# The low halves of layer 2's last float32r operands made by GpSimd or VectorE, in a new planned order

## The chip, the cores and the metric

The kernel runs on one core of one Trainium2 chip. The metric is the device time of one execution in microseconds. The engines are called by the profile's names: PE is TensorE's matmuls and PEld its weight loads, DVE is VectorE, ACT is ScalarE, POOL is GpSimd and SP is SyncE, whose queue issues all DMAs.

## What is computed

Top-32 attention over 4 batches of 8 heads, 576 tokens of 64 dimensions, then two MLPs over the 2304 tokens. All in float32.

```python
def _attn_ref(q, k, v):
    scores = scale * np.matmul(q, k.transpose(0, 1, 3, 2))
    kth = np.partition(scores, -top_k, axis=-1)[..., -top_k:-top_k + 1]
    scores = np.where(scores >= kth, scores, -1000000000.0)
    attn = np.exp(scores - np.max(scores, axis=-1, keepdims=True))
    attn = attn / (np.sum(attn, axis=-1, keepdims=True) + 1e-09)
    return np.matmul(attn, v).astype(np.float32)
...
x = np.ascontiguousarray(attn_out.transpose(0, 2, 1, 3)).reshape(B * S, H * D)   # 2304 x 512
h = x @ w_in                                     # layer 1: 512 -> 2048
x = (h * (1.0 / (1.0 + np.exp(-1.702 * h)))) @ w_out
...
h = x @ w_in                                     # layer 2: 512 -> 2048
P = a[0] + a[1] * h + a[2] * h2 + a[3] * h3      # h2 = h*h, h3 = h2*h
Q = 1.0 + np.abs(b[0]) * np.abs(h) + np.abs(b[1]) * h2
return ((P / (Q + 1e-06)) @ w_out).astype(np.float32)
```

## The kernel before

**Tiles.** The tokens are 18 tiles of 128. A tile has 8 heads, so there are 144 attend steps. One step is: score matmuls into a PSUM buffer S (L678); four MAX8 on DVE (L689) with three MATCH_REPLACE8 between them (L693), which find the 32nd largest value; three ACT passes (L696, L698, L700) and a subtraction on POOL (L702), which make the weights as a high and a low float16 half in A; a transposing DMA from A to AT; and the value matmuls (L721). One small POOL operation per step is L691.

**Layers.** The tiles are grouped in nine granules of two. Layer 1 of a granule runs in units of 512 columns: matmuls into the PSUM buffer h (L860), tanh on ACT (L880), a gate on DVE (L893), halves gh and gl (L917 on ACT, L919 on POOL), and matmuls into acc0 and acc1 (L954). Layer 2's unit has 24 matmuls into h, four ACT passes that read h (L880: Abs, Square and two affine ones), one operation on DVE (L888), Ln and Exp on ACT (L906, L907), three products or sums of two 128x512 tiles on POOL or DVE (L884 is the POOL form, L885 the DVE form of the same line), which give the gate M, and the output matmuls (L951 in plain float32). There is one PSUM buffer for h (NH=1).

**float32r.** For the last two granules (RG = (7, 8)) the output matmuls of layer 2 run in float32r: `round_split` splits the gate tile (names E) and the two weight tiles of a unit (K the high, V the low half) into a rounded high half (L817 on ACT, L818 the DVE form) and the low remainder (L819), and L938 does three matmuls where L951 does one of a slower kind. This makes 16 units with three splits each, 48 in all. They are the last stage of the program.

**Order.** Each engine runs its instructions in the order of the program. `Program.schedule` sets that order: every operation is recorded with an engine, a planned duration and a priority, and perhaps `alt`, another engine that may take it. The planner plays the program through with these durations and picks for each engine the operation that can start first, weighed by its priority and the table OFF. `lock` says that an operation keeps DVE and POOL from running such operations at the same time in the plan. The line that the change is about reads before:

```python
op("DVE", dve(512), lambda: lo(DVE), [rd, hb], [lb], prio, lock=True)
```

`dve(512)` plans 0.6 us for it.

Of the kernel before, what the change touches and what calls it, by code (L numbers as in the profile page):

```python
# [223 lines left out]
def kernel(  # L224
# [20 lines left out]
    NPAIR = DFF // 256  # L245
# [14 lines left out]
    op = pr.op  # L260
# [120 lines left out]
    def w_load(layer, f2, prio):  # L381
        for j in range(2):
# [70 lines left out]
            if layer == 1:  # L453
                dg = buf("dg", [P, P], F32, NDG)
                op("POOL", PDIAG, lambda dg=dg, sc=sc: POOL.tensor_scalar(dg.t, eye, sc, None, ALU.mult), [scb], [dg], prio)
                for c in range(2):
# [6 lines left out]
                    op("PE", 6 * 0.2155, rest, [low, dg, dst], [pl[c]], prio)  # L463
# [21 lines left out]
    def w_consts(layer, prio):  # L485
# [10 lines left out]
        if layer == 1:  # L496
            op("DVE", 1.0, one, [wscale[j, f2] for f2 in range(NPAIR) for j in range(2)], [wcb[1]], prio)
        else:
            op("DVE", 0.15, lambda: DVE.tensor_scalar(sc2, wsi[:, :, 2], im1, 1.0 / CG, ALU.mult, ALU.mult),
               [wcb[1]] + [wscale[2, f2] for f2 in range(NPAIR)], [wcb[2]], prio)  # L500
# [163 lines left out]
    def attend(i, prio):  # L664
# [7 lines left out]
        for r0, n, bb, _ in reversed(sg):  # L672
# [7 lines left out]
            op("PE", 0.49, mm, [qs, K], [s], prio - 1)  # L680
# [129 lines left out]
    def round_split(src, cols, rd, tags, prio):  # L810
# [9 lines left out]
        op("DVE", dve(512), lambda: lo(DVE), [rd, hb], [lb], prio, lock=True)  # L820
# [296 lines left out]
RG = (7, 8)  # L1117
NT0 = 8
# [3 lines left out]
LAV = 0.8762  # L1122
# [11 lines left out]
KLAG = 7.5819  # L1134
QLAG = 3.1885
NKH = 1
NQH = 1
W1P = -0.0003
W2P = 7.8782
W1R = 0.02  # L1140
W2R = 1.0078
LATE = 2
MLAG = 3.5653
SWITCH = 53.68
OLAG = 2.4023
UW = 1.1408
ALATE = -51.37
OFF = {
    ('attend', 'ACT'): 15.52,
    ('attend', 'ACT', 0): -8.51,  # L1150
    ('attend', 'ACT', 1): 15.81,
    ('attend', 'ACT', 2): -8.72,
    ('attend', 'ACT', 3): 6.94,
    ('attend', 'ALT'): 7.89,
    ('attend', 'DVE'): 33.66,
    ('attend', 'DVE', 0): 0.07,
    ('attend', 'DVE', 1): -0.32,
    ('attend', 'DVE', 2): -2.5,
    ('attend', 'DVE', 3): 0.86,
    ('attend', 'PE'): -272.38,  # L1160
    ('attend', 'PE', 0): 3.52,
    ('attend', 'PE', 1): -15.49,
    ('attend', 'PE', 2): 9.83,
    ('attend', 'PE', 3): 17.15,
    ('attend', 'POOL'): 12.13,
    ('attend', 'POOL', 0): -0.38,
    ('attend', 'POOL', 1): -34.1,
    ('attend', 'POOL', 2): 30.8,
    ('attend', 'POOL', 3): -23.18,
    ('attend', 'SP'): -111.84,  # L1170
    ('attend', 'SP', 0): -11.92,
    ('attend', 'SP', 1): 0.05,
    ('attend', 'SP', 2): 8.26,
    ('attend_av', 'ACT'): -323.75,
    ('attend_av', 'ACT', 0): -26.14,
    ('attend_av', 'ACT', 1): 3.65,
    ('attend_av', 'ACT', 2): -17.11,
    ('attend_av', 'ACT', 3): -11.88,
    ('attend_av', 'PE'): -84.87,
    ('attend_av', 'PE', 0): 2.96,  # L1180
    ('attend_av', 'PE', 1): -3.29,
    ('attend_av', 'PE', 2): -12.39,
    ('attend_av', 'PE', 3): -3.81,
    ('k_prep', 'ACT'): 4.12,
    ('k_prep', 'ACT', 0): 14.56,
    ('k_prep', 'ACT', 1): -56.64,
    ('k_prep', 'ACT', 2): 20.72,
    ('k_prep', 'ALT'): 64.83,
    ('k_prep', 'DVE'): 30.23,
    ('k_prep', 'DVE', 0): -43.96,  # L1190
    ('k_prep', 'DVE', 1): -88.43,
    ('k_prep', 'DVE', 2): 22.15,
    ('k_prep', 'DVE', 3): -2.16,
    ('k_prep', 'PE'): 49.18,
    ('k_prep', 'PE', 0): 5.15,
    ('k_prep', 'PE', 1): 5.28,
    ('k_prep', 'PE', 2): 68.78,
    ('k_prep', 'PE', 3): 5.95,
    ('k_prep', 'POOL'): -32.59,
    ('k_prep', 'POOL', 0): 18.63,  # L1200
    ('k_prep', 'POOL', 1): -4.97,
    ('k_prep', 'POOL', 2): -26.89,
    ('k_prep', 'POOL', 3): -30.93,
    ('k_prep', 'SP'): 58.29,
    ('k_prep', 'SP', 0): 6.33,
    ('k_prep', 'SP', 1): -71.47,
    ('k_prep', 'SP', 2): 35.83,
    ('k_prep', 'SP', 3): 17.13,
    ('o_done', 'ACT'): -281.01,
    ('o_done', 'ACT', 0): 2.63,  # L1210
# [254 lines left out]
RATE = 2.25  # L1465
# [32 lines left out]
```

## Time and profile before

| | us |
|---|---|
| median of 3 runs | 1249.11 |
| lowest and highest | 1246.3, 1251.24 |
| the profiled execution | 1240.5 |
| its span, first to last instruction | 1238.8 |
| PE, DVE, ACT, POOL busy in it | 1095.7, 1096.0, 1032.0, 873.2 |

Busy time is a mean over stages with different limits; the rows below cut it by stages. The profiled execution is 8.6 us under the median, so a sum made on the profile is applied to the median as a difference.

### The profile page before, as it was taken

To read this page: it belongs to the slowest core of one execution; us is meant where nothing else is said; L and a number is where in the kernel's file an instruction comes from. 1 tells how busy PE (TensorE), PEld (TensorE's weight loads), DVE (VectorE), ACT (ScalarE), POOL (GpSimd) and SP (SyncE) were. 2 spreads that over 40 slices of the span, in tenths; PEclk is the share of its full clock that TensorE was granted. 3 is DMA by queue.
4 is the path that set the end of the run, shared out by engine and by line. 5 is a ranking of instruction groups with operands and counts; after the bars stand their busy time and mean duration, and the time that the engine had idled before them with its cause. 6 is when DMAs were issued, how large, how long until landed. Compare 5 with 4: busy or idle time off the path is not lost.

```text
span 1238.8 us, 26369 instructions
## 1 busy us (share of the span) xinstructions
PE 1095.7 (88%) x9290; PEld 744.2 (60%) x9290; DVE 1096.0 (88%) x2328; ACT 1032.0 (83%) x1917; POOL 873.2 (70%) x1230
## 2 busy tenths in 40 slices
PE   3867556868898999999989999999999999999997
PEld 2434243645565766676657765756676677677775
DVE  5879999999999999999999999969999999542886
ACT  5888888968888889999988888777889978856886
POOL 6887889886777679777785687556757856422765
PEclk9987678869899999999999999999999999999999
DMA  9949798889889649969695589656956863841651
GB/s 293 259 118 233 221 295 211 218 205 202 181 194 225 112 104 218 208 119 190 152 239 125 119 195 185 125 134 174 189 103 148 202 129 87 208 113 35 190 188 65
DMA packets 363845, 214.08 MB, mean 173 GB/s; under 512 B 316352, under 2 KB 328640, under 8 KB 363712
## 3 DMA queue, kind: packets, MB, share of 16 engines
q1 hardware_dynamic: 363712, 212.39, 71.8%
q8 instruction: 73, 1.20, 0.4%
q14 instruction: 60, 0.49, 0.1%
HBM read 127.93 MB, written 13.11 MB: 114 GB/s over the span
## 4 chain that ended last, share of the span: by engine, by line
PE 46%; DVE 21%; ACT 12%; POOL 8%; DMA 7%; issue 5%; SPq 1%; DVEq 0%; POOLq 0%; ACTq 0%
PE h L860 19%; PE acc L954 9%; PE acc L951 7%; DVE E L693 6%; DVE mx L689 5%; DMA AT<-A 4%; ACT t L880 4%; PE S L678 3%; PE misc L721 3%; POOL t L884 2%; DVE m L689 2%; PE acc L460 2%; PE acc L938 2%; POOL A L702 2%; ACT E L696 1%
## 5 line engine op out<-in xcount | busy, mean ns | idle before, releaser
L689 DVE MAX8 mx<-E 128x8 f32<-128x576 f32 x432 | 321.1, 752 | 3.7
L884 POOL TENSOR_TENSOR t<-t,t 128x512 f32<-128x512 f32 x155 | 211.2, 1363 | 70.6 <-ACT t L880 44.3
L702 POOL TENSOR_TENSOR A<-E,A 128x576 f16<-128x576 f32 x144 | 189.8, 1318 | 50.0 <-ACT A L700 40.7
L951 PE MATMUL acc<-ring,t 128*128 128x512 f32 x448 | 216.3, 608 | 5.3 <-DVE t L885 2.2
L860 PE MATMUL h<-xh,W 128*128 128x128 f16 (+1 forms) x2688 | 212.8, 238 | 6.3 <-DVE t L893 5.8
L693 DVE MATCH_REPLACE8 E<-mx,E 128x576 f32<-128x576 f32 x288 | 213.6, 742 | 0.0
L860 PE MATMUL h<-yh,ring 128*128 128x256 f16 x1728 | 205.0, 274 | 7.3 <-ACT t L880 6.8
L860 PEld LDWEIGHTS <-W 128*128 128x128 f16 x2688 | 192.1, 100 | 32.1 <-issue 12.3
L860 PEld LDWEIGHTS <-ring 128*128 128x128 f16 x1728 | 169.0, 98 | 54.6 <-issue 30.3
L954 PE MATMUL acc<-W,gh 128*128 128x512 f16 x576 | 173.9, 384 | 0.1
L678 PE MATMUL S<-K,qs 128*128 128x288 f16 (+1 forms) x640 | 110.1, 300 | 34.5 <-ACT E L696 32.9
L698 ACT ACTIVATE E<-E,nm,ei 128x576 f32<-128x576 f32 x144 | 124.3, 865 | 8.5 <-POOL nm L697 6.8
L919 POOL TENSOR_TENSOR gl<-t,gh 128x512 f16<-128x512 f32 x72 | 84.5, 1174 | 66.0 <-ACT gh L917 63.7
L689 DVE MAX8 m<-S 128x8 f32<-128x576 f32 x144 | 108.7, 755 | 23.1 <-PE S L678 17.3
L721 PEld LDWEIGHTS <-AT 128*128 128x128 f16 (+3 forms) x2400 | 90.2, 102 | 63.9 <-DMA AT<-A 47.2
L696 ACT ACTIVATE E<-S,mx 128x576 f32<-128x576 f32 x144 | 106.3, 739 | 21.6 <-DVE mx L689 21.2
L721 PE MATMUL misc<-V,AT 128*128 128x65 f16 (+6 forms) x2400 | 98.6, 197 | 28.4 <-DMA AT<-A 26.1
L880 ACT ACTIVATE t<-h,cf 128x512 f32<-128x512 f32 x144 | 93.8, 683 | 31.6 <-PE h L860 30.2
L951 PEld LDWEIGHTS acc<-ring,t 128*128 128x128 f32 x448 | 77.5, 191 | 69.3 <-issue 54.8
L954 PE MATMUL acc<-W,gl 128*128 128x512 f16 x288 | 110.3, 383 | 5.3 <-POOL gl L919 5.1
L678 PEld LDWEIGHTS <-qs 128*128 128x128 f16 (+1 forms) x640 | 63.5, 103 | 79.4 <-issue 60.4
L693 DVE MATCH_REPLACE8 E<-m,S 128x576 f32<-128x576 f32 x144 | 107.6, 747 | 0.0
(186 smaller groups left out, 2062.2 us busy)
## 6 DMA issues: line engine op xcount, KB each, us to landing
ring<-scr SPq DMA_DIRECT2D x144, 512.0 KB, 4.2
ring<-in_moe_w_out_dram SPq DMA_DIRECT2D x12, 1024.0 KB, 6.5
ring<-in_moe_w_in_dram SPq DMA_DIRECT2D x9, 1024.0 KB, 7.1
ld<-in_v_dram SPq DMA_DIRECT2D x32, 256.0 KB, 3.8
out_dram<-t SPq DMA_DIRECT2D x18, 256.0 KB, 2.9
lq<-in_q_dram SPq DMA_DIRECT2D x32, 128.0 KB, 3.4
ld<-in_k_dram SPq DMA_DIRECT2D x16, 256.0 KB, 3.8
yh<-in_moe_w_in_dram SPq DMA_DIRECT2D x4, 1024.0 KB, 6.3
```

Of the source, the lines that this page charges most:

```text
L678: PE.matmul(s[:n, c, :SH], qs[:, 2 * (h % 4) + x, :n], K[:, h % 2, c * SH:(c + 1) * SH], start=(x == 0), stop=(x == 1))
L689: op("DVE", dve(S, not r) + 0.02, lambda r=r, mv=mv: DVE.max(mv(), w.t if r else sv()), [w if r else s], [m], prio)
L693: op("DVE", dve(S, not r) + 0.085, lambda r=r, mv=mv: DVE.match_replace(w.t if r else two(w.t), mv(), w.t if r else sv(), NEG), [m, w if r ...
L696: op("ACT", act(S, True) + APA + 0.02, lambda: ACT.activation(two(e.t), sv(), AF.Prelu, bias=mx[:, 2, 7:8], scale=-1.0, alpha=NEAR), [s, m ...
L698: op("ACT", act(S) + 0.2, lambda: ACT.activation(e.t, e.t, AF.Exp, bias=nm[:, 1:2], scale=eb(0)), [e, nm, ei], [e], prio)
L702: lo = lambda en: en.tensor_tensor(A[:, 1, :S], e.t, A[:, 0, :S], ALU.subtract)
L721: PE.matmul(ps[r0:r0 + n, :hi - lo], at[:kp, x, j, r0:r0 + n], V[:kp, h % 2, j, lo:hi], start=(j == 0 and lo == D and x == 0), stop=(j == ...
L860: PE.matmul(o, w[:, half, kd * 256 + jj * P: kd * 256 + (jj + 1) * P], xy[:, tl, l * ND + kd, :], start=(kd == 0 and n == 0), stop=(kd == ...
L880: op("ACT", act(w, True) + APA, lambda f2=f2, c=c: ACT.activation(dst[:, c], src[:, c], func, bias=bias(f2) if bias else 0.0, scale=sc(f2) ...
L884: op("POOL", pool_tt(512), lambda: POOL.tensor_tensor(o.t, x.t, y.t, f), [x, y], [o], prio, alt=("DVE", dve(512) + 0.04, lambda: DVE.tenso ...
L951: PE.matmul(acc[j].t, u.gate[:, c], w[:, jj * DM:(jj + 1) * DM], start=st, stop=sp)
L954: PE.matmul(acc[j].t, l[:, c], w[:, half, jj * DM:(jj + 1) * DM], start=(st and n == 0), stop=(sp and n == 2))
```

## The change

The lows of `round_split` get a choice: POOL with a planned 1.35 us, or DVE with 1.2 us. Three other planned durations are raised. The planner's table of numbers is replaced as a whole, so that all operations of the program may stand in another order.

```diff
-                    op("PE", 6 * 0.2155, rest, [low, dg, dst], [pl[c]], prio)
+                    op("PE", PREST, rest, [low, dg, dst], [pl[c]], prio)
...
-            op("DVE", 1.0, one, [wscale[j, f2] for f2 in range(NPAIR) for j in range(2)], [wcb[1]], prio)
+            op("DVE", 2.5, one, [wscale[j, f2] for f2 in range(NPAIR) for j in range(2)], [wcb[1]], prio)
...
-            op("PE", 0.49, mm, [qs, K], [s], prio - 1)
+            op("PE", PES, mm, [qs, K], [s], prio - 1)
...
-        op("DVE", dve(512), lambda: lo(DVE), [rd, hb], [lb], prio, lock=True)
+        op("POOL", PLR, lambda: lo(POOL), [rd, hb], [lb], prio, alt=("DVE", DLR, lambda: lo(DVE)))
...
+PLR, DLR, PREST, PES = 1.35, 1.2, 1.6, 0.52
...
-LAV = 0.8762
+LAV = 2.0021
...
-SWITCH = 53.68
+SWITCH = 101.44
...
-    ('u_act2', 'DVE'): -136.15,
+    ('u_act2', 'DVE'): -149.57,
...
-RATE = 2.25
+RATE = 16.09
```

No instruction is added or dropped; some stand on another engine, and most stand elsewhere.

**PE, in the last stage.** h_2120 and h_2131 are the h tiles of the eighth and ninth of the sixteen units; the rows are the end of the one group of matmuls and the beginning of the next. Before, with the last five of the twelve output matmuls between:

```order
L938 MATMUL acc0_69<-V_2130_16181,E_2103_16141 128x512
L938 MATMUL acc0_69<-K_2129_16098,E_2104_16157 128x512
L938 MATMUL acc1_70<-K_2129_16098,E_2103_16141 128x512
L938 MATMUL acc1_70<-V_2130_16181,E_2103_16141 128x512
L938 MATMUL acc1_70<-K_2129_16098,E_2104_16157 128x512
L860 LDWEIGHTS ring_90
L860 MATMUL h_2131_16213<-yh_91,ring_90 128x256
```

After:

```order
L860 MATMUL h_2120_16132<-yh_91,ring_90 128x256
L860 LDWEIGHTS ring_90
L860 MATMUL h_2120_16132<-yh_91,ring_90 128x256
L860 LDWEIGHTS ring_90
L860 MATMUL h_2131_16181<-yh_91,ring_90 128x256
```

The twelve L938 between the two groups stand behind the second one now, in a block of 27.

**POOL, at the end of the program.** t_2202 and t_2213 are the gate tiles of the last two units, V_2209 to V_2228 weight lows of the last four units. Before, the last six rows that compute:

```order
L884 TENSOR_TENSOR t_2202_16658<-t_2202_16658,t_2201_16651 128x512
L884 TENSOR_TENSOR t_2202_16658<-t_2202_16658,t_2203_16665 128x512
L884 TENSOR_TENSOR t_2202_16658<-t_2202_16658,t_2200_16646 128x512
L884 TENSOR_TENSOR t_2213_16722<-t_2213_16722,t_2212_16717 128x512
L884 TENSOR_TENSOR t_2213_16722<-t_2213_16722,t_2214_16728 128x512
L884 TENSOR_TENSOR t_2213_16722<-t_2213_16722,t_2211_16711 128x512
```

After, the last nine:

```order
L819 TENSOR_TENSOR V_2209_16692<-ring_90,K_2208_16540 128x512
L819 TENSOR_TENSOR V_2218_16702<-ring_90,K_2217_16565 128x512
L884 TENSOR_TENSOR t_2213_16704<-t_2213_16704,t_2212_16697 128x512
L884 TENSOR_TENSOR t_2213_16704<-t_2213_16704,t_2214_16709 128x512
L819 TENSOR_TENSOR V_2220_16730<-ring_90,K_2219_16608 128x512
L819 TENSOR_TENSOR V_2222_16736<-ring_90,K_2221_16626 128x512
L819 TENSOR_TENSOR V_2224_16741<-ring_90,K_2223_16668 128x512
L819 TENSOR_TENSOR V_2226_16753<-ring_90,K_2225_16718 128x512
L819 TENSOR_TENSOR V_2228_16761<-ring_90,K_2227_16726 128x512
```

The weight lows came to POOL, five of them behind the last unit's products; the third product of a unit went to DVE.

**DVE, in the middle of the last stage.** t_2132 to t_2134 and t_2143 to t_2145 belong to the ninth and tenth unit. Before:

```order
L888 SCALAR_TENSOR_TENSOR t_2132_16247<-t_2133_16262,ab_76,t_2132_16247 128x512
L885 TENSOR_TENSOR t_2134_16272<-t_2134_16272,t_2133_16262 128x512
L819 TENSOR_TENSOR V_2165_16297<-ring_90,K_2164_16286 128x512
L819 TENSOR_TENSOR E_2126_16318<-t_2123_16201,E_2125_16295 128x512
L888 SCALAR_TENSOR_TENSOR t_2143_16315<-t_2144_16322,ab_76,t_2143_16315 128x512
L819 TENSOR_TENSOR E_2137_16357<-t_2134_16272,E_2136_16339 128x512
L819 TENSOR_TENSOR V_2174_16376<-ring_90,K_2173_16313 128x512
L819 TENSOR_TENSOR V_2176_16396<-ring_90,K_2175_16367 128x512
L888 SCALAR_TENSOR_TENSOR t_2154_16381<-t_2155_16389,ab_76,t_2154_16381 128x512
L819 TENSOR_TENSOR E_2148_16410<-t_2145_16327,E_2147_16398 128x512
```

After:

```order
L888 SCALAR_TENSOR_TENSOR t_2132_16220<-t_2133_16228,ab_76,t_2132_16220 128x512
L885 TENSOR_TENSOR t_2134_16254<-t_2134_16254,t_2133_16228 128x512
L885 TENSOR_TENSOR t_2134_16254<-t_2134_16254,t_2135_16265 128x512
L885 TENSOR_TENSOR t_2134_16254<-t_2134_16254,t_2132_16220 128x512
L888 SCALAR_TENSOR_TENSOR t_2143_16310<-t_2144_16318,ab_76,t_2143_16310 128x512
L885 TENSOR_TENSOR t_2145_16330<-t_2145_16330,t_2144_16318 128x512
L885 TENSOR_TENSOR t_2145_16330<-t_2145_16330,t_2146_16334 128x512
L885 TENSOR_TENSOR t_2145_16330<-t_2145_16330,t_2143_16310 128x512
```

Here the six lows went to POOL, and all three products of a unit came to DVE.

## Rows read from the trace of the kernel before

**Rows 1.** The page: busy time, and PE's granted clock in 40 slices.

```profile
PE 1095.7 (88%) x9290; PEld 744.2 (60%) x9290; DVE 1096.0 (88%) x2328; ACT 1032.0 (83%) x1917; POOL 873.2 (70%) x1230
...
PEclk9987678869899999999999999999999999999999
```

**Rows 2.** Busy time in stretches: us, PE, PEld, DVE, ACT, POOL, clock, DMA share, GB/s.

```profile
44.00:768.20 724.20, 619.13 (x5382) 413.81 (x5380) 691.27 (x1591) 632.11 (x1208) 570.57 (x837) 0.92 0.81 188
768.20:1052.40 284.20, 279.38 (x2527) 190.94 (x2528) 261.70 (x524) 234.94 (x422) 182.32 (x251) 1.00 0.66 145
1052.40:1130.00 77.60, 77.60 (x694) 52.78 (x693) 34.60 (x54) 51.15 (x96) 25.27 (x25) 1.00 0.49 129
1130.00:1239.00 109.00, 97.54 (x611) 74.62 (x608) 82.12 (x90) 85.78 (x144) 64.82 (x45) 1.00 0.40 136
```

**Rows 3.** What writes m, in one stretch (DVE, POOL); then what uses S.

```profile
768.20:1052.40 284.20, 63.22 (x121) 14.77 (x40) 1.00 0.66 145
...
L678 PE MATMUL S<-K,qs x640: 282/286/448, 42.9 to 1051.5; 128*128 128x288 f16 x144, 128*64 128x288 f16 x16
```

**Rows 4.** Timeline of PE in the last stage: start, us, line, tiles, count [idle before].

```profile
1155.24 2.78 PE L860 MATMUL h<-yh,ring 128*128 128x256 f16 x24
...
1160.71 2.78 PE L860 MATMUL h<-yh,ring 128*128 128x256 f16 x24 [1.29 <-ACT t L880]
...
1178.11 2.78 PE L860 MATMUL h<-yh,ring 128*128 128x256 f16 x24
...
1184.71 2.78 PE L860 MATMUL h<-yh,ring 128*128 128x256 f16 x24 [1.03 <-ACT t L880]
...
1189.36 0.74 PE L938 MATMUL acc<-K,E 128*128 128x512 f32 x2 [1.39 <-DVE E L819]
...
1203.42 2.78 PE L860 MATMUL h<-yh,ring 128*128 128x256 f16 x24 [0.61 <-ACT t L880]
```

**Rows 5.** Timeline of ACT between two of those groups.

```profile
1181.51 0.71 ACT L906 ACTIVATE t<-t,kc 128x512 f32<-128x512 f32 x1
...
1182.69 0.62 ACT L907 ACTIVATE t<-t 128x512 f32<-128x512 f32 x1
```

**Rows 6.** Timeline of DVE and POOL; two groups of 1130 to 1239 us: busy, mean ns, idle.

```profile
1154.63 0.68 DVE L819 TENSOR_TENSOR V<-ring,K 128x512 fp32r<-128x512 f32 x1
...
1157.11 1.77 DVE L819 TENSOR_TENSOR V<-ring,K 128x512 fp32r<-128x512 f32 x1
...
1142.96 1.28 POOL L884 TENSOR_TENSOR t<-t,t 128x512 f32<-128x512 f32 x1 [4.59 <-ACT t L880]
...
1154.59 8.68 POOL L884 TENSOR_TENSOR t<-t,t 128x512 f32<-128x512 f32 x5 [2.36 <-ACT t L880]
1163.71 1.29 POOL L884 TENSOR_TENSOR t<-t,t 128x512 f32<-128x512 f32 x1 [0.43 <-ACT t L907]
...
L884 POOL TENSOR_TENSOR t<-t,t 128x512 f32<-128x512 f32 x41 | 62.4, 1522 | 30.9 <-ACT t L880 21.0 <-ACT t L907 6.9 <-ACT K L817 0.7
...
L919 POOL TENSOR_TENSOR gl<-t,gh 128x512 f16<-128x512 f32 x1 | 1.2, 1153 | 4.1 <-ACT gh L917 4.1
```

**Rows 7.** Timeline of the end: POOL's last products, PE's last matmul, the store.

```profile
1225.93 4.67 POOL L884 TENSOR_TENSOR t<-t,t 128x512 f32<-128x512 f32 x3 [0.56 <-ACT t L880]
...
1234.61 0.40 PE L938 MATMUL acc<-K,E 128*128 128x512 f32 x1
...
1234.97 1.03 SPq L1018 DMA_DIRECT2D out_dram<-t  x2
```

**Rows 8.** The chain that ended last: two of its pieces.

```profile
1035.54 2.62 PE h L860 x24
...
1129.84 2.59 PE acc L954 x12
```

**Rows 9.** DVE's waits, from 44 to 350 us and from 350 to 1090: us, times, longest.

```profile
DVE m L689 <- PE S L678: 8.2, 7, 3.2
...
DVE m L689 <- PE S L678: 9.1, 16, 1.8
```

More of the change, by code (lines that the diff above doesn't have):

```diff
@@ L1133 @@
 VLO = 0
[L1134 to L1135 removed]
+KLAG = 7.3553
+QLAG = 3.5241
 NKH = 1
 NQH = 1
[L1138 to L1141, printed above, removed]
+W1P = -0.5495
+W2P = 7.2247
+W1R = 0.672
+W2R = 0.9283
 LATE = 2
[L1143 to L1454 removed]
@@ L1464 @@
 WIN = {'DVE': 0.0, 'ACT': 0.0, 'POOL': 0.0, 'PE': 0.0, 'SP': 0.0}
-RATE = 2.25
-PHASES = (-4.4, 44.0, 122.3)
+RATE = 16.09
+PHASES = (-2.0, 44.1, 122.4)
 FREE = ("t", "misc", "sum", "p2", "wl")
```

557 lines of the change are left out of this document (314 added, 243 removed).

## The prediction

> **What bounds the kernel now.** I read the page first, then the time cut into stages, then the last stage instruction by instruction. The page says that PE and DVE are both busy for 88% of the span and that PE's clock is low only early [rows 1]. That is an average over unlike stages. I cut the span at the 104th attend step (768 us), at the last one (1052 us) and where the float32r units begin (1130 us) [rows 2].
>
> - Up to 768 us DVE is busy for 691.27 of 724.20 us (95.5%) and PE for 619.13. DVE with its top-k passes sets the pace.
> - From 768 to 1052 us forty attend steps run, which the count of L691 shows, and the last score matmul stands at 1051.5 us [rows 3]. PE is busy for 279.38 of 284.20 us (98.3%), DVE for 261.70 (92.1%). PE sets the pace, DVE stands 6% behind.
> - From 1052 to 1130 us PE is never idle and DVE is busy for 34.60 of 77.60 us.
> - From 1130 us on run the sixteen units of layer 2 for granules 7 and 8, the only place with the operations that the change moves. PE is busy for 97.54 of 109 us; DVE for 82.12, POOL for 64.82. PE is the engine to watch there too, and its idle time is what the change can win or lose.
>
> What makes PE idle in that last stage is seen in its own rows [rows 4]. There is one PSUM buffer h. After the 24 matmuls of a unit, ACT reads h four times (L880), and only then may the next 24 start. The group at 1155.24 ends at 1158.02, the next starts at 1160.71: 2.69 us. Six output matmuls (L938) stand between and cover 1.40 us; 1.29 us are idle, released by ACT L880. With nine between, 0.61 us are idle (before 1203.42). With twelve (2.8 us) nothing is, unless ACT does something else between its four reads: at 1181.51 and 1182.69 it does L906 and L907 in between [rows 5], and the next group starts 3.82 us after the end of the last (1180.89 to 1184.71) with 1.03 us idle. So each such insertion costs (3.82 - 2.69)/2 = 0.56 us. DVE's lows released PE once in that stage for more than half a microsecond: 1.39 us at 1189.36.
>
> **The change part by part.**
>
> *The lows themselves.* Of the 48 low halves (L819), all on DVE before, 39 stand on POOL now and 9 on DVE. Four of those 39 come ahead of the last stage in both orders, so I count 35 moved within it. In return the gate products (L884 on POOL, L885 on DVE) go the other way: POOL had 41 in the last stage [rows 6] and has 21, DVE had 7 and has 27. ACT takes twelve more of the high halves (L817, 34 to 46).
>
> *What they cost.* A DVE low alone takes 0.68 us (at 1154.63), next to a POOL product 1.77 us (at 1157.11); a POOL product alone takes 1.29 us (at 1163.71), and five in a row with DVE in between take 8.68 us, 1.74 each [rows 6]. So they take turns: a POOL operation holds about 1.29 us and a DVE operation with two operands about 0.45 more. A low on POOL has not run here. From below it may cost the 1.15 us of POOL's low of float16 (L919, [rows 6]), from above the 1.52 us that the products average in this stage. I take 1.3 us, since it has the products' operands and size. The Trainium skill ("SBUF — State Buffer", Who interferes with whom) says that a VectorE instruction with two SBUF inputs and a GpSimd instruction that reads SBUF exclude each other for a whole instruction. By that rule, and the trace agrees, a low that goes to POOL frees nothing on the shared port but holds it longer; the rival below works this out. In sums: before, 41 x 1.29 + 69 x 0.45 = 84 us of turns (69 is 44 lows, 16 L888, 7 L885 and 2 L995 on DVE); after, 56 x 1.29 + 54 x 0.45 = 97 us. In the forecast these turns still lie beside PE's matmuls, because POOL and DVE run ahead of PE by a unit or two.
>
> *PE's order in the last stage.* Here I count with the rule read above: 2.7 us from the end of one group to the start of the next, 0.56 for each insertion on ACT, less what stands between. Before: 6 matmuls once (1.3), 9 twice (0.6 each), 12 with two insertions twice (1.0 each), 12 with one insertion twice (0.5 each), in all 5.5 us. After: three L954 only, 0.65 us of cover (2.05); 12 with one insertion (0.5); 9 (0.6); 9 with two insertions (1.7); nothing at all between h_2120 and h_2131 (2.7); 12 with two (1.0); 6 (1.3). In all 9.9 us. The term is **+4.4 us**.
>
> *Waits for lows.* The wait of 1.39 us at 1189.36 need not return: **-1.4 us**. The new places have little reserve. From the seventh unit on POOL has 23 operations in a row; the 21st ends, at 1.29 us each and 0.45 for each of some 15 DVE turns, 34 us after the first begins. PE gets to its use after six groups of 2.55 us, 66 matmuls of 0.233 and 3.7 us of the gaps counted above, also 34 us. I book nothing for it and take 0 to 6 us as its bounds.
>
> *The end.* Before, POOL's last three products start at 1225.93 and take 4.67 us; then a low on DVE, PE's last matmul starts at 1234.61 and the store at 1234.97 [rows 7]. After, POOL has two products of the last unit and behind them five weight lows, and PE's last five matmuls cannot go before the last of them. 1225.93 + 2 x 1.56 + 5 x 1.3 = 1235.5, then 0.15 for the handover and five matmuls of 0.23 us, so 1236.9 against 1235.0: **+1.9 us** (3.2 if a low takes 1.56).
>
> *The order ahead of it.* Up to the 104th attend step both orders put the same work on PE and DVE, step for step within a few microseconds, and the lag from score to value matmuls is three steps for most heads in both: **0**, with 5 us either way. From there to the last step it differs: behind the last score matmul stand 960 matmuls of L860 now, 888 before, and 135 of L954, 96 before. At 2.62 us for 24 and 2.59 for 12 [rows 8] these are 7.9 + 8.4 = 16.3 us of PE work that now follows the attend steps. PE's share of the window from 768 to 1052 falls to 263 us. If PE keeps pacing it the window shrinks by 16.3 and the sum is **0**. For that DVE has to put 258 us (three L885 fewer stand ahead of the last step, and some 2 us of small work elsewhere) into 268, 96.3%, a little above its 95.5% up to 768 us. If it reaches only 94%, the window takes 274 and 6 to 7 us are lost. That is the bound above; below nothing.
>
> *Costs in the table* (PREST, PES, the 2.5 of w_consts) execute nothing; they only shaped the order.
>
> **Sum.** 4.4 - 1.4 + 1.9 = +4.9 us. The profiled execution took 1240.5 us with a span of 1238.8; the runs shown have a median of 1249.11. I add the 4.9 us to the median: **1254 us**, 0.4% more. What a measurement of this kernel can tell from no change is about 0.5%, here 6.2 us.
>
> **The rivals.**
>
> 1. *POOL becomes the bound of the last stage* (slower). Its first product of the stage starts at 1142.96 [rows 6]. If turns alone filled its time from there it would end at 1142.96 + 97 = 1240, and as above the last matmuls (1.4 us) and the store (1238.8 - 1235.0 = 3.8) follow, 1245 against 1238.8: +6.5. POOL now idles for 30.9 us of that stage, waiting for ACT [rows 6]; if a fifth of that stays, +13. Together with the end of the attend steps falling short by 4 us the time is 1249 + 13 + 4 = 1266. For it: POOL's rows of 1.74 us beside DVE. Against it: five of the units give POOL nothing but lows, which have no chain to wait for. It decides from POOL's lows at 1.45 us on.
>
> 2. *The new order takes DVE's waits out* (faster). DVE waits for score matmuls 8.2 us from 44 to 350 us and 9.1 us from 350 to 1090 [rows 9]. If most of that went, 12 of 17.3 us, and the last stage lost only the 4.9, the time would be 1242; with all of it 1237. It decides from 11 us on. For it: layer 1's first units stand earlier in PE's order (180 matmuls of L860 ahead of the 16th score now, 48 before), so PE's queue is better filled. Against it: by the 24th score both have done the same, 99 and 100 us of PE work.
>
> 3. *The change does nothing:* PE's idle time in the last stage is refilled as units slide, and 16.3 us come back whole: 1249.
>
> **How the numbers follow.** The forecast and rival 3 lie within 0.5%, though the forecast is near its edge, and a loss of 2 us at the end of the attend steps carries it over. Forecast 0.45, a third of it (0.15) beyond the edge; rival 1 0.20; rival 2 0.22; rival 3 0.13, of which 0.02 ends beyond the edge by the 5 us left open up to the 104th step. That gives faster 0.22, within 0.5% 0.30 + 0.11 = 0.41, slower 0.15 + 0.20 + 0.02 = 0.37. The forecast alone spans 1249 to 1260. The range takes rival 2 in part and rival 1 whole: 1240 to 1266.
>
> **What would show it.** Right: PE idle 2 to 3 us between the two groups without matmuls between; PE's idle time from 1130 on about 4 us more; the last attend step at 1036 to 1040 us; the last instruction before the store a matmul that waited for POOL L819. Wrong: PE waiting for POOL L819 in the middle of the stage (rival 1); the 104th step earlier than 768 by over 8 us (rival 2); lows on POOL far from 1.3 us, or PE's gaps after 2.7 us failing to appear.

## The result and the profile after

The changed kernel takes 1263.16 us (median of six runs, 1261.33 to 1267.86), the kernel before 1246.46 in the same comparison. The ratio is 1.0138, interval 1.0109 to 1.0166: **1.4% slower, 17 us**, against the 0.4% forecast. Below, "us over before" is the ratio less one, times 1245.

The page of the changed kernel, busy time and granted clock, answers to [rows 1]:

```profile
PE 1094.6 (87%) x9290; PEld 748.1 (59%) x9290; DVE 1090.0 (86%) x2302; ACT 1036.3 (82%) x1929; POOL 893.1 (71%) x1244
...
PEclk9887787869989999999999999999999999999999
```

Nearly the same busy time on PE, DVE and ACT, in a span that is 22 us longer (1261.1); POOL has 20 us more. Its stretches, as in [rows 2], cut at the 104th step, the last step and ahead of the float32r units:

```profile
43.00:781.00 738.00, 619.24 (x5360) 417.50 (x5359) 699.29 (x1590) 629.49 (x1204) 569.66 (x837) 0.92 0.79 182
781.00:1051.00 270.00, 264.72 (x2439) 180.65 (x2438) 255.09 (x520) 224.39 (x408) 176.30 (x249) 1.00 0.71 152
1051.00:1144.00 93.00, 93.00 (x797) 63.11 (x796) 37.14 (x61) 63.19 (x115) 28.75 (x28) 1.00 0.43 116
1144.00:1261.00 117.00, 97.19 (x613) 74.89 (x610) 71.21 (x66) 90.41 (x153) 86.09 (x60) 1.00 0.39 126
```

The second stretch is 14 us shorter than in [rows 2], the third 15 longer: the output and h matmuls moved behind the last step, as forecast. In the last stretch PE is idle for 19.8 of 117 us, against 11.5 of 109 [rows 2], and POOL is busy for 86.09 instead of 64.82.

PE's timeline at the place with nothing between two h groups, and POOL's at the same time:

```profile
1189.17 2.78 PE L860 MATMUL h<-yh,ring 128*128 128x256 f16 x24 [1.74 <-ACT t L880]
1194.64 2.78 PE L860 MATMUL h<-yh,ring 128*128 128x256 f16 x24 [2.69 <-ACT t L880]
```

```profile
1188.01 2.94 POOL L884 TENSOR_TENSOR t<-t,t 128x512 f32<-128x512 f32 x2 [2.05 <-ACT t L880]
1191.43 1.27 POOL L884 TENSOR_TENSOR t<-t,t 128x512 f32<-128x512 f32 x1 [0.48 <-ACT t L907]
1192.66 6.31 POOL L819 TENSOR_TENSOR V<-ring,K 128x512 fp32r<-128x512 f32 x4
```

The 2.69 us are those of [rows 4] with no cover. POOL's rows show why there was nothing to put there: the weight lows that the next output matmuls need start at 1192.66, behind three products of a later unit that waited for ACT. The end has the same shape; POOL's last rows, and PE's wait for the first of the five lows at 1248.52:

```profile
1239.22 3.04 POOL L884 TENSOR_TENSOR t<-t,t 128x512 f32<-128x512 f32 x2 [1.00 <-ACT t L880]
1242.21 2.97 POOL L819 TENSOR_TENSOR V<-ring,K 128x512 fp32r<-128x512 f32 x2
1245.14 3.42 POOL L884 TENSOR_TENSOR t<-t,t 128x512 f32<-128x512 f32 x2
1248.52 7.15 POOL L819 TENSOR_TENSOR V<-ring,K 128x512 fp32r<-128x512 f32 x5
```

```profile
1249.83 0.50 PE L938 MATMUL acc<-V,E 128*128 128x512 f32 x1 [2.93 <-POOL V L819]
```

### The profile page after: what moved, and what is told of

The parts are those of the page before. It is cut to its first block, busy times and chain, and to the rows that moved or that the text cites. A ratio compares the mean times of both kernels' runs of the same rounds, so it can differ in the third digit from the quotient of the medians.

```text
span 1261.1 us, 26420 instructions
## 1 busy us (share of the span) xinstructions
PE 1094.6 (87%) x9290; PEld 748.1 (59%) x9290; DVE 1090.0 (86%) x2302; ACT 1036.3 (82%) x1929; POOL 893.1 (71%) x1244
## 4 chain that ended last, share of the span: by engine, by line
PE 39%; DVE 21%; ACT 12%; DMA 10%; POOL 10%; issue 6%; SPq 1%; POOLq 0%; DVEq 0%; ACTq 0%
PE h L860 17%; PE acc L954 7%; PE acc L951 6%; DVE E L693 6%; DMA AT<-A 5%; DVE mx L689 5%; ACT t L880 4%; PE S L678 3%; PE misc L721 3%; POOL A L702 2%; DVE m L689 2%; POOL t L884 2%; DMA qs<-qh 2%; PE acc L938 2%; DVE ring L420 1%
## 5 line engine op out<-in xcount | busy, mean ns | idle before, releaser
L860 PEld LDWEIGHTS <-W 128*128 128x128 f16 x2688 | 195.6, 102 | 50.3 <-issue 29.6
L884 POOL TENSOR_TENSOR t<-t,t 128x512 f32<-128x512 f32 x130 | 173.4, 1334 | 40.2 <-ACT t L880 27.7
L696 ACT ACTIVATE E<-S,mx 128x576 f32<-128x576 f32 x144 | 106.3, 738 | 33.3 <-DVE mx L689 29.1
L721 PE MATMUL misc<-V,AT 128*128 128x65 f16 (+5 forms) x2400 | 100.5, 198 | 35.8 <-DMA AT<-A 27.9
L721 PEld LDWEIGHTS <-AT 128*128 128x128 f16 (+2 forms) x2400 | 90.9, 103 | 68.5 <-DMA AT<-A 49.5
L689 DVE MAX8 m<-S 128x8 f32<-128x576 f32 x144 | 108.6, 755 | 14.8 <-PE S L678 13.9
L880 ACT ACTIVATE t<-h,cf,cf 128x512 f32<-128x512 f32 x144 | 105.5, 781 | 0.0
```

The costliest lines, as they stand in the source:

```text
L689: op("DVE", dve(S, not r) + 0.02, lambda r=r, mv=mv: DVE.max(mv(), w.t if r else sv()), [w if r else s], [m], prio)
L696: op("ACT", act(S, True) + APA + 0.02, lambda: ACT.activation(two(e.t), sv(), AF.Prelu, bias=mx[:, 2, 7:8], scale=-1.0, alpha=NEAR), [s, m ...
L721: PE.matmul(ps[r0:r0 + n, :hi - lo], at[:kp, x, j, r0:r0 + n], V[:kp, h % 2, j, lo:hi], start=(j == 0 and lo == D and x == 0), stop=(j == ...
L860: PE.matmul(o, w[:, half, kd * 256 + jj * P: kd * 256 + (jj + 1) * P], xy[:, tl, l * ND + kd, :], start=(kd == 0 and n == 0), stop=(kd == ...
L880: op("ACT", act(w, True) + APA, lambda f2=f2, c=c: ACT.activation(dst[:, c], src[:, c], func, bias=bias(f2) if bias else 0.0, scale=sc(f2) ...
L884: op("POOL", pool_tt(512), lambda: POOL.tensor_tensor(o.t, x.t, y.t, f), [x, y], [o], prio, alt=("DVE", dve(512) + 0.04, lambda: DVE.tenso ...
```

## The experiments

In most of them the planner's order is replaced by one written out, which names for every recorded operation its place and engine (from the kernel before, the changed one, or either with an edit):

```diff
-    order = pr.schedule(SWITCH)
+    order = []
+    for n in ORDER:
+        o = pr.ops[n >> 1]
+        if n & 1:
+            o.eng, o.dur, o.fn = o.alt
+        order.append(o)
```

All results in one table. "Step 100" is the start of its first MAX8 in the profile, "h 1" that of the first h group of the sixteen units, "stage" the time from there to the end of the span. Steps are counted from 0. The start of step 100 differs by up to 12 us between profiles of one order; the stage repeats within 0.2 us in the order of before.

| kernel | ratio to before | interval | us over before | step 100 | h 1 | stage |
|---|---|---|---|---|---|---|
| before | 1 | | 0 | 748.1 | 1132.3 | 106.5 |
| after | 1.0138 | 1.0109-1.0166 | 17.2 | 757.6 | 1146.7 | 114.4 |
| last_of_after | 1.0091 | 1.0069-1.0113 | 11.3 | 745.6 | 1132.0 | 117.4 |
| last_of_before | 1.0061 | 1.0042-1.0080 | 7.6 | 751.1 | 1138.2 | 106.3 |
| front_b100_rest_a | 1.0112 | 1.0089-1.0135 | 13.9 | 751.7 | 1139.2 | 118.4 |
| front_a100_rest_b | 1.0055 | 1.0033-1.0076 | 6.8 | 760.0 | 1144.5 | 106.5 |
| swap_alone | 1.0070 | 1.0041-1.0099 | 8.7 | 749.2 | 1133.6 | 116.3 |
| order_alone | 1.0123 | 1.0094-1.0151 | 15.3 | 759.0 | 1146.4 | 113.4 |
| groups_apart | 1.0123 | 1.0101-1.0144 | 15.3 | 752.8 | 1140.1 | 117.1 |
| lows_first | 1.0106 | 1.0079-1.0133 | 13.2 | 747.9 | 1135.9 | 113.6 |
| later_on_dve | 1.0184 | 1.0161-1.0207 | 22.9 | 770.2 | 1155.4 | 114.9 |
| mended | 1.0162 | 1.0134-1.0190 | 20.2 | 763.7 | 1152.1 | 112.7 |
| bare_pairs | 1.0115 | 1.0088-1.0143 | 14.3 | 749.0 | 1133.5 | 117.7 |
| choice_alone | 1.0178 | 1.0152-1.0203 | 22.2 | 754.2 | 1138.9 | 122.0 |
| table_alone | 1.0047 | 1.0023-1.0072 | 5.9 | 757.0 | 1144.1 | 107.6 |
| costs_alone | 1.0133 | 1.0110-1.0156 | 16.6 | 760.4 | 1150.8 | 106.5 |
| lows_only | 1.0156 | 1.0123-1.0188 | 19.4 | 754.3 | 1138.4 | 125.4 |
| rest_only | 1.0017 | 0.9992-1.0042 | 2.1 | 757.5 | 1141.5 | 108.1 |
| nine_back | 1.0122 | 1.0091-1.0154 | 15.2 | 759.9 | 1147.6 | 112.5 |

**Where the loss lies.** Four orders, each made of one kernel's first part and the other's rest:

```diff
-order: the planner's
+last_of_after:     before's to the first h group of the last stage, then after's
+last_of_before:    after's to that group, then before's
+front_b100_rest_a: before's to the score matmuls of step 100, then after's
+front_a100_rest_b: after's to those, then before's
```

> The order is written out: every engine follows the order (and the choice of engine) of the kernel before up to the first h group of the last stage, and from there that of the changed kernel, with its lows on GpSimd. In the two profiles the stretch from that first h group to the end is 106.4 us before (1132.43 to 1238.8) and 114.4 us after (1146.70 to 1261.1). Theory A (the loss has two sources: some 8 us in the last stage by its own order and lows, the rest by the planner's other order far ahead of it): 1246.5 + 8 = 1254.5 us. Rival B (all of the loss is the lows on GpSimd and the last stage): 1263 us. Rival C (all of the loss is in the order ahead of it, and the last stage is worth nothing): 1246.5 us.

> The mirror image: the order of the changed kernel up to the first h group of the last stage, and from there the order of the kernel before, with 44 of the lows on VectorE. Theory A: 1263.2 - 8 = 1255 us. Rival B: 1246.5 us. Rival C: 1263 us. If the two mirror images add up, their two differences to the kernel before sum to the 16.7 us between the two kernels.

> The order of the kernel before up to the score matmuls of attend step 100, from there that of the changed kernel with its last stage. In the profiles the first MAX8 of step 100 starts at 748.1 us before and at 757.6 us after, 9.5 us apart. Theory A (the order between the 40th and the 100th step loses some 9 us, which nothing behind it gives back): 1263.2 - 9.5 = 1254 us. Rival B (all of it is in the last stage): 1263 us, as the changed kernel. A result at 1247 us would mean that the front is the whole loss.

> The mirror image: the order of the changed kernel up to the score matmuls of attend step 100, from there that of the kernel before, last stage too. Theory A: 1246.5 + 9.5 = 1256 us, with no low on GpSimd in the last stage. Rival B: 1246.5 us.

Both pairs add up within their intervals (18.9 and 20.7 against 17.2). Theory A holds, B and C fall: some 11 us lie in the last stage, some 7 ahead of it. At step 100 theory A was too high: its 9.5 us came from one pair of profiles. Over eight profiles of each order the start of step 100 is at 751.2 and 755.7 us on average (4.5 apart), and from there to the first h group it takes 384.6 and 387.7. The difference of 4.5 us at step 100 is the mean of starts that spread by 12 us in either order, so it is known to within some 4 to 5 us only; the timed front_a100_rest_b puts the part ahead of step 100 at 6.8 (4.1 to 9.5). The last stage takes 106.5 us in four profiles of the order of before and 116.3 on average in four of the changed one (114.4 to 118.4).

That spread is a thing that the sum had not held: PE's clock. PE's timeline in front_b100_rest_a, and the windows' row of that stretch (the granted clock stands third from the right):

```profile
1150.48 4.45 PE L860 MATMUL h<-yh,ring 128*128 128x256 f16 x24 [2.05 <-ACT t L880]
...
1187.48 4.38 PE L860 MATMUL h<-yh,ring 128*128 128x256 f16 x24 [2.69 <-ACT t L880]
```

```profile
1150.50:1157.50 7.00, 7.00 (x37) 5.50 (x37) 5.01 (x10) 4.63 (x9) 2.03 (x3) 0.76 0.23 77
```

Behind the idle 2.05 and 2.69 us the same 24 matmuls take 4.4 us instead of 2.78. The mean granted clock of the 7 us shown is 0.76; from 1151 to 1154 us it is 0.50, the lower of the two levels (1.2 GHz instead of 2.4). In the profile of the changed kernel the same two gaps are followed by 2.78, at a granted clock of 1.00.

**Lows or order, in the last stage.**

```diff
-order and engines: the planner's
+swap_alone:  before's order, 73 operations of the last stage on after's engines
+lows_only:   before's order, of these 73 only the 39 lows (to POOL)
+rest_only:   before's order, of these 73 only the other 34
+order_alone: after's order, these 73 on before's engines
```

> The order of the kernel before in everything, the last stage too; only the 73 operations of the last stage that stand on another engine in the changed kernel (lows to GpSimd, products to VectorE and the like) are put on that engine, at the same place of the order. Theory Q (what costs the last stage its 8 us and more is GpSimd: its queue is in order and slow, and the lows land too late for the output matmuls): the stage loses 8 to 11 us, 1252 to 1255 us against 1244 in this comparison, and TensorE waits at L938 for lows of GpSimd. Rival O (it is the new order of TensorE in the stage, the groups of h matmuls with nothing between): at most the 3.5 us of the end, 1244 to 1248 us.

> The mirror image: the order of the changed kernel in everything, but the operations of the last stage on the engines of the kernel before (lows on VectorE, products on GpSimd). Theory Q: the end is as before (17.8 us from the last h group instead of 21.2), the lows are early; TensorE's gaps that the order fixes stay, about 9 us against 4.4. So some 5 us of 1263 come back, 1257 to 1259. Rival O: only the end comes back, 1260 us. If the swap were all, the last stage would be as before: 1252 us.

> The order of the kernel before; 39 lows stand on GpSimd, at the same place of the order, and all products stay where they were. GpSimd then has 35 lows and 41 products in the last stage: 76 x 1.29 us and some 34 turns of VectorE of 0.45 us, 113 us from the first at 1143, and the last one ends at 1256 at best instead of 1231 in that profile. Theory K (GpSimd's capacity): 20 us and more over the kernel before, 1265 us. Theory Q (only the late places cost): about as swap_alone, 8 to 10 us more, 1253 to 1256.

> The order of the kernel before with all 48 lows on VectorE; only the other 34 operations of the last stage that changed engine (products to VectorE, high halves to ACT) stand where the changed kernel has them. Both theories: VectorE has room (12 of 20 us busy), so within 2 us, 1244 to 1248. If this alone loses as much as swap_alone (8.7 us), the lows are not the cause.

The lows cost; what the rest costs (rest_only, 2.1 us) can't be told from nothing. lows_only came out as its theory K had it, 1264.84 us: POOL was full, as its windows show (the fifth busy time), and PE's timeline has waits for it:

```profile
1163.00:1183.00 20.00, 15.82 (x104) 12.35 (x104) 10.68 (x8) 15.40 (x27) 19.77 (x15) 1.00 0.63 179
1183.00:1203.00 20.00, 16.24 (x98) 11.95 (x97) 6.44 (x5) 12.71 (x22) 19.92 (x15) 0.91 0.39 125
1203.00:1223.00 20.00, 16.84 (x97) 12.96 (x98) 5.23 (x5) 13.41 (x23) 19.92 (x16) 0.91 0.47 171
1223.00:1243.00 20.00, 15.30 (x93) 11.44 (x91) 12.02 (x9) 13.89 (x24) 19.84 (x15) 1.00 0.23 79
```

```profile
1195.60 0.80 PE L938 MATMUL acc<-V,E 128*128 128x512 f32 x1 [1.49 <-POOL V L819]
...
1204.65 0.72 PE L938 MATMUL acc<-K,E 128*128 128x512 f32 x2 [2.28 <-POOL E L819]
```

With the other 34 operations moved as well, 20 of them products given to DVE (swap_alone), the loss falls from 19.4 to 8.7 us. But order_alone fell out against theory Q: with the lows back on DVE the changed order loses 15.3 us, nearly what the changed kernel does. The 1260.5 us are rival O's number, but not for its reason: the end did not come back. From the last h group on it takes 20.7 us (17.7 before, 21.2 changed), with PE waiting 2.00 and 1.53 us for lows that now stand on DVE. So the changed order of the stage is late by itself, whichever engine makes the lows; that the planner made it so because it planned for late lows is likely, but not shown by this run.

**Mending the changed kernel.** groups_apart moves twelve matmuls on PE; lows_first also moves seven lows on POOL; nine_back has the move on PE and gives nine weight lows to DVE. The core of each, as it stands on PE, POOL and DVE:

```diff
 L860 h_2120 x24
+L938 x12 (second half of unit 5, first half of unit 6)
 L860 h_2131 x24
-L938 x12
```

```diff
+L819 V x2
 L884 t x2   (first two products of the seventh unit)
+L819 V
 L884 t      (its third product)
-L819 V x3
```

```diff
-POOL L819 V x9   (the second low of units 5 to 9 and 13 to 16)
+DVE  L819 V x9
```

> The changed kernel; on TensorE alone twelve output matmuls (the second half of the fifth unit, the first half of the sixth) are moved from behind the ninth h group to the place between the eighth and the ninth, where nothing stood and 2.69 us were idle. In the profile of the changed kernel the two weight lows that they need end at 1193.9 and 1195.6, and the eighth group ends at 1192.0. Theory Q: TensorE waits there for GpSimd's lows instead; the ninth group starts 2 to 2.5 us later than it did, and the time is unchanged, 1262 to 1263. Rival O: 2.7 us are won, 1260.5; then the idle time was the order's.

> As groups_apart, and on GpSimd seven weight lows stand ahead of products that they stood behind: two ahead of the seventh unit's first product, one ahead of its third, and one or two each ahead of the third product of the fourteenth unit and of the products of the fifteenth and sixteenth. In the profile of the changed kernel those products wait 2.05, 0.48, 0.23, 1.22 and 1.00 us for ACT, with the lows behind them, whose sources were there for up to 14 us. Engines, ACT and VectorE are as in the changed kernel. Theory Q (the in-order queue of GpSimd): the gap of 2.69 us closes and the end comes 2.5 to 3 us earlier, 1257 to 1258. Rival C (GpSimd is simply full): the lows only change places, 1262 to 1263. Rival O: 1260.5, from the groups alone.

> The changed kernel with the twelve output matmuls in the empty place (groups_apart), and nine weight lows (the second ones of units 5 to 9 and 13 to 16) on VectorE instead of GpSimd, each behind the first one of its unit in the order. This takes 12 us of GpSimd's work away. Theory K: the last stage takes 108 to 110 us instead of 114 to 118 and the time is 1257. Theory Q: GpSimd's remaining lows still stand behind the products, the end and the K,E waits stay, 1260 to 1262 us.

The timeline of PE in groups_apart:

```profile
1186.80 0.50 PE L938 MATMUL acc<-V,E 128*128 128x512 f32 x1 [1.79 <-POOL V L819]
...
1190.80 3.12 PE L860 MATMUL h<-yh,ring 128*128 128x256 f16 x24
```

The 2.69 us became a wait for POOL of 1.79, with 0.54 us for ACT and 0.73 for POOL a little later, as theory Q had it; in time it can't be told from the changed kernel. lows_first closed the gap (no wait ahead of the ninth group), but 0.53 and 0.74 us behind it stayed and 1.72 came at the end; its stage, 113.6 us, holds one group at the lower clock of 4.45 us. Without that, and in mended without such a group (112.7), it is 1.7 to 2.5 us under the 114.4 of the changed kernel, less than half of what Q said. Its time, 1257.5 us, is Q's number (1257 to 1258), but its interval overlaps that of the changed kernel. nine_back took some 12 us of work from POOL (nine lows of 1.3), and its stage, 112.5 with one group of 4.24, is not much shorter; 1261.4 us are Q's number, not K's. POOL's capacity is not the limit of the changed kernel.

**Idle places alone, in the order of before.**

```diff
-L938 x12 of unit 4, L860 of group 7;  of unit 6, group 9;  of unit 11, group 14
+L860 of group 7, L938 x12 of unit 4;  group 9, unit 6;     group 14, unit 11
```

> The kernel before; on TensorE alone the twelve output matmuls ahead of the 7th, the 9th and the 14th h group of the last stage stand behind that group, so that three pairs of groups have nothing between, as the changed kernel has once. Lows stay on VectorE. Theory G (a bare place costs its 2.69 us of idle time, and TensorE's clock may fall to half behind it for one group, which takes 4.1 to 4.4 us instead of 2.78): three gaps of 2.7, less the gaps of 0.43, 1.03 and 1.03 us and the wait of 1.39 us that the fuller places take away, so 4 to 5 us more, and up to 1.5 us more for each drop of the clock. Rival N (the idle time is refilled behind, as units slide): no change, 1244 to 1246 us.

PE's timeline at the first two pairs:

```profile
1167.88 4.16 PE L860 MATMUL h<-yh,ring 128*128 128x256 f16 x24 [3.13 <-ACT t L880]
...
1178.83 2.78 PE L860 MATMUL h<-yh,ring 128*128 128x256 f16 x24 [0.93 <-ACT t L880]
1184.30 2.78 PE L860 MATMUL h<-yh,ring 128*128 128x256 f16 x24 [2.69 <-ACT t L880]
...
1194.20 2.78 PE L860 MATMUL h<-yh,ring 128*128 128x256 f16 x24 [1.56 <-ACT t L880]
```

Theory G in kind, not in size: the stage is 11.2 us longer, not 4 to 5. Each bare place costs 2.7 to 3.1, the clock fell once, and behind the 24 output matmuls that follow a pair, 5.6 us of cover, the next group still waits 0.93 and 1.56 for ACT. A place that is left empty is not paid back by the fuller one behind it.

**The front.** later_on_dve moves three instructions of DVE; mended is that with lows_first.

```diff
-L781 of tile 7; L888 of granule 2, unit 2; L551 of q tile 11, half 2
+the same three, four, three and four instructions later on DVE
```

> The changed kernel; on VectorE alone three instructions stand three or four places later: the reciprocal L781 of tile 7, L888 of a layer-2 unit (granule 2, second unit) and L551 of a q tile (tile 11, second half). In all profiles of the changed kernel's front VectorE waits 1.4 to 1.7, 1.3 to 1.5 and 1.8 to 2.0 us at these three for a result of ACT, with MAX8 and MATCH_REPLACE8 behind them that have all they need; the front of the kernel before has no such wait. Theory W (the new order puts VectorE's instructions ahead of their operands, in the stretch where VectorE sets the pace): from step 36 to step 100 the profile takes 426 to 427 us instead of 430 to 432, and the time falls by 4 to 5 us to 1258. Rival S (VectorE then waits for score matmuls instead, since TensorE is nearly as busy): 430 us and 1263 us.

> later_on_dve and lows_first together in the changed kernel: three instructions later on VectorE, twelve output matmuls in the empty place on TensorE, seven weight lows earlier on GpSimd; engines and everything else as in the changed kernel. lows_first alone came out some 4 us under the changed kernel. Theory W: 1263.2 - 4 - 4.5 = 1254.5 us, half of the loss undone by moving 22 of 7060 recorded operations. Rival S: as lows_first, 1259 us.

DVE's waits between steps 36 and 100 (us, times, longest), before:

```profile
DVE m L689 <- PE S L678: 5.5, 9, 1.2
DVE t L893 <- ACT t L880: 2.3, 2, 1.3
```

in the changed kernel:

```profile
DVE m L689 <- PE S L678: 6.1, 8, 2.2
DVE qh L551 <- ACT qh L634: 3.2, 3, 2.0
DVE r L781 <- ACT x L730: 2.3, 3, 1.5
DVE t L888 <- ACT t L880: 1.7, 2, 1.3
```

and in later_on_dve:

```profile
DVE m L689 <- PE S L678: 12.4, 13, 2.1
DVE t L893 <- ACT t L880: 4.8, 2, 2.9
DVE t L888 <- ACT t L880: 3.7, 5, 1.4
DVE qh L551 <- ACT qh L634: 3.6, 3, 2.1
```

Theory W fell. The new waits of the front are real, but moving the instructions three or four places back made the kernel 5.7 us slower than the changed one, and mended 7.0 us slower than lows_first. In the profile of later_on_dve (1272.0 us, the median is 1267.5) the wait for score matmuls has doubled, and L893 waits 4.8 us where it waited 0.7 in the changed kernel. The three waits can't be taken away by themselves; which chain of engines they end was not followed up.

**Choice, table and planned durations apart.**

choice_alone, on the kernel before (with PLR, DLR = 1.35, 1.2):

```diff
-        op("DVE", dve(512), lambda: lo(DVE), [rd, hb], [lb], prio, lock=True)
+        op("POOL", PLR, lambda: lo(POOL), [rd, hb], [lb], prio, alt=("DVE", DLR, lambda: lo(DVE)))
```

table_alone is the changed kernel with this line put back as it was:

```diff
-        op("POOL", PLR, lambda: lo(POOL), [rd, hb], [lb], prio, alt=("DVE", DLR, lambda: lo(DVE)))
+        op("DVE", dve(512), lambda: lo(DVE), [rd, hb], [lb], prio, lock=True)
```

costs_alone, on the kernel before:

```diff
-                    op("PE", 6 * 0.2155, rest, [low, dg, dst], [pl[c]], prio)
+                    op("PE", 1.6, rest, [low, dg, dst], [pl[c]], prio)
...
-            op("DVE", 1.0, one, [wscale[j, f2] for f2 in range(NPAIR) for j in range(2)], [wcb[1]], prio)
+            op("DVE", 2.5, one, [wscale[j, f2] for f2 in range(NPAIR) for j in range(2)], [wcb[1]], prio)
...
-            op("PE", 0.49, mm, [qs, K], [s], prio - 1)
+            op("PE", 0.52, mm, [qs, K], [s], prio - 1)
```

> The kernel before with the line of the change alone: the lows have the choice between GpSimd (1.35) and VectorE (1.2); the table of numbers and the other planned durations stay. The planner then puts 19 of the 48 lows on GpSimd, and the order is that of the kernel before up to the last stage. swap_alone, with 35 of them on GpSimd, lost 8.7 us. Theory E (a low on GpSimd is late because it stands in order behind products that wait for ACT): a part of that, 2 to 5 us, 1247 to 1250, with TensorE's waits at L938. Rival F (it is the number of lows on GpSimd that makes it full, and 19 of them fit): 1244 to 1246 us.

> The changed kernel with the line of the lows as it was before: all 48 lows on VectorE with a planned 0.6 us, under the new table and the new durations. The order up to the last stage is that of the changed kernel, and the last stage is planned anew. Theory T (the new front costs some 7 us and the choice the rest): 1252 to 1253 us if its last stage is as good as that of the kernel before, as last_of_before was. Theory X (the square adds up: choice alone +22, both +17): the table alone would win 5 us, 1240. Rival L (the table makes a late last stage whoever does the lows, as order_alone): 1260.

> The kernel before with the three raised planned durations alone (1.6 us for the two matmuls of L460 and L461, 2.5 for the constants, 0.52 for a score group); the table stays, no low moves, and no instruction executes differently but by its place. Theory B (an order that was found for one set of durations is spoiled by any other, in many small waits): slower by 4 to 10 us. Rival N (they only shift the plan, the order stays good): 1244 to 1247 us.

choice_alone missed both theories by far: 22.2 us with 19 of 48 lows on POOL, 122.0 in the stage, where PE is idle for 23.6 us (11.2 before), nearly half of that ahead of h groups; why the planner orders it so badly was not looked into. table_alone is near theory T, if a little under it: without the choice the new order costs 5.9 us, and its newly planned last stage (107.6) is about as good as that of before. costs_alone loses 16.6 us, more than theory B said, and all of it ahead of a last stage that is unchanged (106.5): three durations that execute nothing. So the durations cost 16.6 us under the old table, the new table brings that to 5.9, and the choice adds 11.3 to it. No version was found that beats the kernel before.

## Why the prediction was wrong

The forecast, 4.9 us and so hardly to be told from no change, was too low; the kernel lost 17.2. With the profiles' means the parts are 4.5 + 3 + 9.8 = 17.3, and two steps failed. The order ahead of the last stage was put at 0 and cost 7.5 us, the larger part of the 12.4 that were missed; the last stage was put at +4.9 and cost 9.8.

- **"Up to the 104th attend step ... 0, with 5 us either way":** +4.5 at step 100, inside the bound. What in the order costs it is open. "They only shaped the order" was said of the raised durations, and no term was booked for that shape; alone, under the old table, it costs 16.6 us (costs_alone).
- **The work moved behind the last step, 0, with 6 to 7 us as the bound:** from step 100 to the last step 13.0 us less (304.0 to 291.0), forecast 16.3; from there to the first h group 16.0 more (80.6 to 96.6), forecast 16.3. So +3. In the profile of the changed kernel DVE is busy for 94.5% of that stretch (255.09 of 270), near the bound's 94%, where 96.3% were needed. Both zeros had bounds that held; that both would come out on the slow side was not foreseen.
- **The last stage, +4.9: the step whose mechanism failed.** It measured +9.8 (106.5 to 116.3), in the timed runs some 11 (17.2 less table_alone's 5.9; last_of_after 11.3). Over the four profiles of either order the 9.8 are 5.0 of idle time ahead of h groups, 2.3 of waits at L938 and 2.5 of PE's busy time.
  - *PE's order, +4.4*: in the profile of the changed kernel the idle time ahead of h groups over 0.25 us rose from 4.39 to 10.73 us, +6.3. The rule from [rows 4] is right for single places: 2.05, 0.43, 1.74, 2.69 and 1.03 came where it put 2.05, 0.5, 1.7, 2.7 and 1.0. It missed others: 1.39 came for 0.6, 0.66 and 0.75 were not in the list, and its 1.3 ahead of the last group did not come; for the kernel before it had 5.5 where 4.39 are.
  - *Waits for lows, -1.4, and "I book nothing for it"*: the wait of 1.39 us did go, but the waits at L938 rose in all from 2.87 to 5.32, +2.5, where this term and the end together had +0.5. Ahead of the last h group they are 1.73 for 1.39; behind it, where PE waits 0.66 and 2.93 for POOL's weight lows, 3.59 for 1.48. "In the forecast these turns still lie beside PE's matmuls, because POOL and DVE run ahead of PE by a unit or two" does not hold once lows stand on POOL behind products that wait for ACT.
  - *The clock* was not in the sum. PE's busy time in the stage is 95.2 us on average in the order of before; in the changed one it is 94.5 where no group ran at the lower clock and 95.7, 99.3 and 101.0 in the other three profiles: 1 to 6.5 us.
  - *The end, +1.9*: right in size for the waits (3.59 less 1.48 is 2.1), not in its reason. It had PE's last five matmuls wait for the last of POOL's five lows. PE waits for the first of them, which ends at 1249.78, and then runs without a wait: the last low ends at 1255.67 and the last five matmuls start at 1255.99 with no idle time ahead of them. (From the last h group to the end it takes 21.2 us instead of 17.7; six more output matmuls stand there.)

The rows of PE's idle time in the stage that are not shown above; before:

```profile
1172.63 2.78 PE L860 MATMUL h<-yh,ring 128*128 128x256 f16 x24 [0.43 <-DMA ring<-scr]
...
1215.56 2.78 PE L860 MATMUL h<-yh,ring 128*128 128x256 f16 x24 [1.03 <-ACT t L880]
...
1227.09 0.50 PE L938 MATMUL acc<-K,E 128*128 128x512 f32 x1 [0.48 <-ACT E L817]
...
1229.52 0.50 PE L938 MATMUL acc<-V,E 128*128 128x512 f32 x1 [0.26 <-DVE V L819]
...
1231.32 0.50 PE L938 MATMUL acc<-K,E 128*128 128x512 f32 x1 [0.38 <-ACT E L817]
...
1232.41 0.73 PE L938 MATMUL acc<-K,E 128*128 128x512 f32 x2 [0.36 <-DVE E L819]
```

and in the changed kernel:

```profile
1158.04 2.78 PE L860 MATMUL h<-yh,ring 128*128 128x256 f16 x24 [2.05 <-ACT t L880]
...
1169.79 2.78 PE L860 MATMUL h<-yh,ring 128*128 128x256 f16 x24 [0.43 <-ACT t L880]
...
1176.03 2.78 PE L860 MATMUL h<-yh,ring 128*128 128x256 f16 x24 [0.66 <-ACT t L880]
...
1182.30 2.78 PE L860 MATMUL h<-yh,ring 128*128 128x256 f16 x24 [1.39 <-ACT t L880]
...
1204.42 2.78 PE L860 MATMUL h<-yh,ring 128*128 128x256 f16 x24 [0.75 <-ACT t L880]
...
1217.13 2.78 PE L860 MATMUL h<-yh,ring 128*128 128x256 f16 x24 [1.03 <-ACT t L880]
...
1237.36 0.50 PE L938 MATMUL acc<-K,E 128*128 128x512 f32 x1 [1.02 <-ACT E L817]
...
1238.82 0.74 PE L938 MATMUL acc<-K,E 128*128 128x512 f32 x2 [0.71 <-DVE E L819]
...
1243.53 0.50 PE L938 MATMUL acc<-V,E 128*128 128x512 f32 x1 [0.66 <-POOL V L819]
```

The rest of what was forecast:

- **The price of a low on POOL, 1.3 us**: weight lows took 1.25 to 1.30 alone and 1.7 beside DVE's two-operand work, 1.52 in the mean of all 39. Right; it was the use of this price that failed, not the price. That the two take turns agrees with the Trainium skill ("SBUF — State Buffer", Who interferes with whom), by which a VectorE instruction with two SBUF inputs contends with a GpSimd instruction that reads SBUF.
- **Rival 1 (POOL becomes the bound, 1266)** came nearest in time. Its mechanism is shown for the lows without the exchange (lows_only), but in the changed kernel relief of POOL wins little (nine_back). What binds there is the order of the stage: with the lows on DVE it loses as much (order_alone), while a stage that is planned for lows on DVE loses 1 us (table_alone). The price of POOL reached the time through the plan.
- **Rivals 2 and 3** fall: DVE's waits for score matmuls did not go (5.5 and 6.1 us between steps 36 and 100), and nothing was refilled (bare_pairs).
- **The signs**: the 2.69 us between the two h groups came. PE's idle time in the last stage rose by 8.7 us (11.2 to 19.9), not 4, and the last step came at 1051 us in the profile, not 1036 to 1040: the 104th step was 13 us late there.

Not settled: which of the many moves costs the front its 4.5 us (later_on_dve shows that it is not the three waits that stand out), how much of the timed loss of the last stage is the clock, since only profiles show it, and why the stage of choice_alone takes 122 us.

## What to carry to other kernels

Where one engine's queue is filled with work from two chains, cost an added instruction by what stands ahead of it and what that waits for, not by its duration and the engine's free time. Count an idle place of PE at its full length, with nothing given back behind it, and add a bound for the clock. And when a planner's durations change, expect the whole order to change: measure the durations, the table and the choice apart, since here they gave +16.6, -10.7 and +11.3 us in this order, and the choice by itself, under the old table, +22.2.

## What the runs showed of the hardware

An idle place of TensorE can cost 1.3 to 1.7 us more in the clock behind it, and not in every run: behind idle times of 2.04 to 3.13 us a group of 24 h matmuls took 4.12 to 4.45 us instead of 2.78 in ten of 21 such places of all profiles, and 2.78 in the other eleven, with the same gaps. Waits at L938 did it as well: six more groups took 3.12 to 4.16 us, four shortly behind waits of 1.49 to 2.28 us and two behind waits of 1.03 and 0.7 us close together; behind the same two waits four other groups took 2.79. In the four profiles with the last stage of before, where no gap is over 1.4 us, no group did, and the granted clock is 1.00 up to PE's last matmul.
